# One-hots read from PSUM, first-expert tiles on two PSUM tiles, and a denser order of the last routing, in a retention and mixture-of-experts kernel

## The chip, the cores and the metric

The kernel runs on one core of a Trainium2 chip. The metric is the device time of one execution in microseconds, the median of the runs. A core has five engines that run side by side, each through its own list of instructions in order: TensorE (PE, with its weight loads PEld), VectorE (DVE), ScalarE (ACT), GpSimd (POOL) and SyncE (SP, which here only starts transfers).

## The reference

The kernel computes a retention layer and, from its output, a mixture of experts with two experts per token.

```python
B, H, S, D = 8, 8, 576, 64
scores = q @ k^T / sqrt(D)
gamma = 1 - 2 ** (-5 - h)                    # per head
ret = scores * where(i >= j, gamma ** (i - j), 0)
x = (ret @ v), as rows of 4608 tokens x 512
noisy = x @ w_gate + log1p(exp(x @ w_noise)) * noise      # 4608 x 8
top2 = the two largest of noisy per token; weights = softmax of those two
out[token] = sum over its two experts e: weight * (relu(x @ w1[e]) @ w2[e])   # 512 -> 1024 -> 512
```

## The kernel before

The work has three stages that overlap. **Attention** runs over 16 units (a unit is one batch, four heads), `n` from 0 to 16: unit `n` gets its scores while unit `n-1` gets its output (`out`). A unit's scores go through the PSUM tile `S` in two halves, each multiplied by a mask on DVE (L269) into SBUF. `cast` turns the loaded keys and queries into bf16 on POOL (`kn` at L199, `qb` at L207), two units ahead; `tr` transposes them on PE (L249); `states` (L288) writes the PSUM tile `T`. SP loads the units four ahead (L176, L181).

**Routing** works on 1152 tokens (two batches) at a time, four routings (`bp` from 0 to 3). `Router.route` is a generator: each `yield` ends a piece, and the main loop puts one piece between two parts of a unit (`step`). A routing computes the logits (PSUM tile `R`, L500), takes the two largest on DVE, counts ranks (running sums `cum` on POOL at L561, matmuls L600 and L602 into `R`), writes the token rows `xr` to DRAM (`xd`), and then builds the list of tokens for each slot of each expert: `olo` (L653) and `oh` (L657) are one-hot masks that DVE makes by comparing a row of column counts, `iota16` (0 to 127, f16, in SBUF), with numbers of each token. 18 matmuls (L668) of `oh` with `olo` add up the list in `R`. `finish` (L697, L698) makes `xi` of it, the row numbers for the gathers.

**Experts**: a tile is 256 slots of one expert. POOL gathers its two halves by an indirect transfer (`xd` by `xi`), PE transposes it, multiplies by `w1` (g1) and by `w2` (g2), and the result goes to `yd` or, with the token's first result added, to `out`. Five tiles whose slots are full early run ahead, in the generator `early` ("first-expert tiles" here, tile 0 to 4; L389 transposes, L398 g1 into the PSUM tile `S`, L402 relu on ACT, L411 g2, L414 the scaled copy `y`). They borrow the buffers `raw_q`, `raw_k`, `raw_v` of the attention loads, four of each name. Each g1 has eight column blocks of 128; a tile of `S` holds four. `early` yields after each relu and each g2 half, and one of its steps follows each piece of the last routing; it starts when three routings are done. Three of its tiles need two routings, the other two need three.

The 35 late tiles run in `experts`. The first three use `raw_q` buffers too (`pre`, L1214, L840), the others seven buffers `xg`. The buffers `xg` and `prv` (the token's first result) are set to zero once on DVE at the start of `experts` (L862, L864). The late tiles' small arithmetic (`small`, L920 to L931) stands on DVE ahead of the relu (L966); L943 transposes, L959 is their g1 and L979 their g2.

All five engines run in an order written out by hand (`manual_schedule`): instructions stand on each engine as the program emits them, so a late piece holds up what stands behind it.

Of the kernel before, what the change touches and what calls it, by code (L numbers as in the profile page):

```python
# [9 lines left out]
F16 = mybir.dt.float16  # L10
F32 = mybir.dt.float32
# [4 lines left out]
Act = mybir.ActivationFunctionType  # L16

P = 128
N = 4608
NCOL = N // P  # L20
E = 8
# [29 lines left out]
def constants(nc, cp):  # L51
    K = {}
    K["ident"] = cp.tile([P, P], BF16, name="ident")
    make_identity(nc, K["ident"])
    K["ones"] = cp.tile([P, P], BF16, name="ones")
    nc.vector.memset(K["ones"], 1.0)
    K["ltri"] = cp.tile([P, P], BF16, name="ltri")
    nc.vector.memset(K["ltri"], 1.0)
    nc.gpsimd.affine_select(K["ltri"], K["ltri"], pattern=[[1, P]], base=0, channel_multiplier=-1,
                            compare_op=Alu.is_gt, fill=0.0)  # L60
    K["iota"] = cp.tile([P, P], BF16, name="iota")
    nc.gpsimd.iota(K["iota"], pattern=[[1, P]], base=0, channel_multiplier=0,
                   allow_small_or_imprecise_dtypes=True)
    K["iota16"] = cp.tile([P, P], F16, name="iota16")
    nc.gpsimd.iota(K["iota16"], pattern=[[1, P]], base=0, channel_multiplier=0,
                   allow_small_or_imprecise_dtypes=True)
    K["local"] = cp.tile([P, NC9], F32, name="local")
    nc.gpsimd.iota(K["local"], pattern=[[P, NC9]], base=1, channel_multiplier=1,
                   allow_small_or_imprecise_dtypes=True)
    K["pidx"] = cp.tile([P, 1], F32, name="pidx")  # L70
    nc.gpsimd.iota(K["pidx"], pattern=[[0, 1]], base=0, channel_multiplier=1,
                   allow_small_or_imprecise_dtypes=True)
    K["desc"] = cp.tile([P, E], F32, name="desc")
    nc.gpsimd.iota(K["desc"], pattern=[[-1, E]], base=E, channel_multiplier=0,
                   allow_small_or_imprecise_dtypes=True)

    K["mask"] = cp.tile([P, 2, P], BF16, name="mask")
    nc.vector.memset(K["mask"], 1.0)
    for h in range(2):
        for rs in range(2):  # L80
            m = K["mask"][h * HD:(h + 1) * HD, rs, :].rearrange("p (r q) -> p r q", r=4)
            nc.gpsimd.affine_select(m, m, pattern=[[1, 4], [4, 32]], base=-rs, channel_multiplier=-2,
                                    compare_op=Alu.is_ge, fill=0.0)
    K["maskt"] = cp.tile([P, 2, HD], BF16, name="maskt")
    nc.vector.memset(K["maskt"], 0.0)
    for b in range(2):
        m = K["maskt"][b * HD:(b + 1) * HD, b, :]
        nc.vector.memset(m, 1.0)
        nc.gpsimd.affine_select(m, m, pattern=[[1, HD]], base=0, channel_multiplier=-1,
                                compare_op=Alu.is_ge, fill=0.0)  # L90

    K["tok"] = cp.tile([P, 4, NC9], F32, name="tok")
    for r in range(4):
        for b in range(2):
            nc.gpsimd.iota(K["tok"][r * 32:r * 32 + 32, :, 4 * b:4 * b + 4], pattern=[[1152, 4], [P, 4]],
                           base=r + 576 * b, channel_multiplier=4, allow_small_or_imprecise_dtypes=True)
    for h in range(2):
        t = K["tok"][h * HD:(h + 1) * HD]
        nc.gpsimd.iota(t[:, :, 8:9], pattern=[[1152, 4], [0, 1]], base=576 * h + 512, channel_multiplier=1,
                       allow_small_or_imprecise_dtypes=True)  # L100
    K["cols"] = cp.tile([P, NCOL], BF16, name="cols")
    nc.gpsimd.iota(K["cols"], pattern=[[1, NCOL]], base=1, channel_multiplier=0,
                   allow_small_or_imprecise_dtypes=True)

    K["cap"] = cp.tile([P, 3, E], F32, name="cap")
    for j, t in enumerate((CAPA, CAPB, ROW0)):
        for e in range(E):
            nc.gpsimd.memset(K["cap"][:, j, e:e + 1], float(t[e]))
    return K
# [250 lines left out]
def early(tc, K, at, keep, xd, yd, W, tiles, routed):  # L360
# [30 lines left out]

    def g1(i, fp):
        w = W[tiles[i][1]]
        p1 = at.ps.tile([P, 4, TS], F32, name="S", bufs=1)
        for f4 in range(4):
            for di in range(KD):
                o = di * F + (4 * fp + f4) * P
                nc.tensor.matmul(p1[:, f4, :], lhsT=w[:, o:o + P], rhs=st[i]["xT"][:, di, :],  # L398
                                 start=(di == 0), stop=(di == KD - 1))
            if f4 % 2:  # L400
                f = 4 * fp + f4 - 1
                nc.scalar.activation(st[i]["hT"][:, f:f + 2, :], p1[:, f4 - 1:f4 + 1, :], Act.Relu)  # L402
                yield

    def g2(i, s):
        n, e, t = tiles[i]
# [11 lines left out]

    for _ in range(3):
        gather(0)  # L420
    yield
    transp(0)
    yield
    for i in range(len(tiles)):
        for fp in range(KF // 4):
            for _ in g1(i, fp):
                gather(i)
                yield
        for s in range(2):
            if not s and i + 1 < len(tiles):  # L430
                while len(st) == i + 1:
                    yield
                    gather(i)
                transp(i + 1)
                yield
            g2(i, s)
            gather(i)
            yield


class Router:
    def __init__(self, tc, ctx, K, at, wgn, moe_noise, xd, keep):
# [11 lines left out]
        self.moe_noise = moe_noise  # L454
        self.w = self.one.tile([P, 2, NCOL], F32, name="w_all")
        self.ov = self.one.tile([P, 2, NCOL], F32, name="ov_all")

        self.fill = self.one.tile([P, 2, E], F32, name="fill")
        nc.vector.memset(self.fill, 0.0)
# [20 lines left out]
    def route(self, bp):  # L480
# [13 lines left out]
            nc.scalar.activation(xr[c // 3][:, c % 3, :DM // 2].bitcast(BF16), pt, Act.Copy)  # L494


        pg = ps.tile([P, C, 2, 2 * E], F32, name="R", bufs=1)
        for c in range(C):
            for di in range(KD):
                nc.tensor.matmul(pg[:, c].rearrange("p s e -> p (s e)"), lhsT=xT[:, di, c, :],  # L500
# [95 lines left out]
        G.tensor_copy(pl[:, :, 3], K["tok"][:, bp])  # L596
        yield
        row(6)
        pr = ps.tile(SH, F32, name="R", bufs=1)
        nc.tensor.matmul(pr.rearrange("p c a e -> p (c a e)"), lhsT=K["ltri"],  # L600
                         rhs=M.rearrange("p c a e -> p (c a e)"), start=True, stop=False)
        nc.tensor.matmul(pr.rearrange("p c a e -> p (c a e)"), lhsT=K["ones"],  # L602
# [47 lines left out]
        oh = sp.tile([P, 2, C, NH], F16, name="oh", bufs=1)  # L650
        for j in range(2):
            sh = [P, C, P]
            V.tensor_tensor(olo[:, j], K["iota16"].unsqueeze(1).to_broadcast(sh),  # L653
                            lo[:, j].unsqueeze(2).to_broadcast(sh), Alu.is_equal)
            yield
            for c in range(C):
                V.tensor_scalar(oh[:, j, c, :], K["iota16"][:, :NH], hi[:, j, c:c + 1], K["local"][:, c:c + 1],  # L657
                                Alu.is_equal, Alu.mult)
                if c == 4:
                    yield  # L660
            yield
        for a, t in ((self.keep["key"], rc.rearrange("p c a -> p a c")), (self.w, w), (self.ov, ov)):
            G.tensor_copy(a[:, :, c0:c0 + C], t)
        yield
        pT = ps.tile([P, NH], F32, name="R", bufs=1)
        for j in range(2):
            for c in range(C):
                nc.tensor.matmul(pT, lhsT=olo[:, j, c, :], rhs=oh[:, j, c, :],  # L668
# [16 lines left out]

    def counts(self, n):

        pn = self.at.ps.tile([P, 2, E], F32, name="R", bufs=1)
        self.nc.tensor.matmul(pn.rearrange("p a e -> p (a e)"), lhsT=self.K["ones"],
                              rhs=self.cum[:, n * NC9].rearrange("p a e -> p (a e)"), start=True, stop=True)  # L690
        return pn
# [153 lines left out]
def experts(tc, K, wp, w1, w2, keep, xd, yd, out, W, pre):  # L845
# [7 lines left out]
    with tc.tile_pool(name="moe_g", bufs=1) as gp, \  # L853
# [4 lines left out]
         tc.tile_pool(name="moe_ps", bufs=1, space=bass.MemoryType.PSUM) as ps:  # L858
        xgs = [gp.tile([P, 2, XW], F32, name=f"xg{j}") for j in range(NX)]
        prv = [gp.tile([P, 2, DM], F32, name=f"prv{j}") for j in range(NP)]  # L860
        for j in range(NX):
            nc.vector.memset(xgs[j], 0.0)  # L862
        for j in range(NP):
            nc.vector.memset(prv[j], 0.0)  # L864
        st = {}
        writes = []
        parts = {}
# [115 lines left out]

        def prev(i, s):
            if i < NT and seconds(i)[s]:
                rows = ROW0[LATE[i][0]]
                nc.gpsimd.indirect_dma_start(  # L987
                    out=prv[i % NP][:, s, :], out_offset=None, in_=yd[:rows, :],
                    in_offset=IOff(ap=st[i]["ix"][:, s, 1:2], axis=0),
                    bounds_check=rows - 1, oob_is_err=False)  # L990
# [40 lines left out]

        with tc.manual_schedule(engines=order):
            for i in range(len(pre), 5):
                for s in range(2):
                    gather(tc, keep, xd, xgof(i), i, s)
            small(0)
# [9 lines left out]
            for i in range(NT + 1):  # L1046
# [12 lines left out]
                if i + 1 >= NT:  # L1059
                    comb(i - 1)  # L1060

                for s in range(2):
                    if i + 5 < NT:
                        gather(tc, keep, xd, xgof(i + 5), i + 5, s)
# [28 lines left out]
def kernel(  # L1093
# [27 lines left out]
    with ExitStack() as actx, tc.manual_schedule(engines=order):  # L1121
# [21 lines left out]
            while work and next(work[0], work) is work:  # L1143
                work.pop(0)

        def step():
            while pend and next(pend[0], pend) is pend:
                pend.pop(0)
                routed.append(0)
                if len(routed) == 3:  # L1150
                    work.append(early(tc, K, at, keep, xd, yd, W, EARLY, routed))
            if n == NU:
                more()

# [6 lines left out]
        for n in range(NU + 1):  # L1161
# [40 lines left out]
                at.tr_tail((u + 1) // 4)  # L1202
            if n in (11, 12, 13, 14):
                load_weights(nc, wp, moe_w1, moe_w2, (n - 11) // 2, W, (n - 11) % 2)
            if n == NU - 1:
                more()
        while pend:
            step()
        rt.finish()

# [42 lines left out]
```

## Time and profile before

| What | us |
|---|---|
| Median of 3 runs | 531.49 (530.38 to 531.77) |
| Profiled execution, its time | 530.18 |
| Profiled execution, span of the trace | 528.3 |
| PE busy | 424.9 (80%) |
| ACT busy | 282.6 (53%) |
| POOL busy | 274.4 (52%) |
| DVE busy | 261.4 (49%) |
| L657 `oh`, 72 instructions, mean | 0.542 |
| L398 g1 of first-expert tiles, PE idle before it | 10.1 |

The page shows busy tenths of each engine in 40 slices of the span (13.2 us each). A timeline line reads: start, busy time, engine, line, operation, output and inputs with shapes, how many; in brackets how long the engine stood idle before it and what released it. Times in timelines count from the start of the span. Where several instructions of a line follow each other, they are shown as one with their number. The loop over the late tiles fills the span from about 257 us to 511 us.

### The profile page before, as it was taken

How to read it: one execution, taken by the hardware profiler on the slowest of the kernel's cores; microseconds unless marked ns; L12 is line 12 of the kernel's file. 1: busy time of each engine (PE TensorE's matmuls, PEld its weight loads, DVE VectorE, ACT ScalarE, POOL GpSimd, SP SyncE). 2: the span in 40 equal slices, each digit the busy share in tenths (PEclk: the TensorE clock that was granted, in tenths of full speed). 3: DMA queues.
4: the chain of work that ended last, by engine and by line, in shares of the span. 5: the costliest groups of instructions: out<-in, count | busy, mean ns of one | idle time of the engine just before them, and what ended most of it. 6: DMA issues, size and time to landing. Idle time of an engine off the chain costs nothing.

```text
span 528.3 us, 11736 instructions
## 1 busy us (share of the span) xinstructions
PE 424.9 (80%) x4627; PEld 304.3 (58%) x4627; DVE 261.4 (49%) x695; ACT 282.6 (53%) x429; POOL 274.4 (52%) x379
## 2 busy tenths in 40 slices
PE   0477677477277758787999999999999999999960
PEld 0365555366266535564767676676666776666630
DVE  4343298868956854724233433424434354444440
ACT  3487597398449326544456666575655744322200
POOL 3783357327733153508505571744747767777440
PEclk9998677686767658999999999999999999999995
DMA  8996899992853821334677698697797864645330
GB/s 245 261 241 167 211 241 308 255 309 57 181 86 61 174 55 59 96 106 113 212 254 254 229 302 280 216 338 227 274 348 249 293 242 141 205 157 176 134 125 2
DMA packets 96169, 104.19 MB, mean 197 GB/s; under 512 B 25447, under 2 KB 73064, under 8 KB 96112
## 3 DMA queue, kind: packets, MB, share of 16 engines
q1 hardware_dynamic: 79824, 69.51, 44.2%
q0 software_dynamic: 14176, 32.83, 22.3%
q10 hardware_dynamic: 2112, 1.08, 0.7%
q8 instruction: 37, 0.61, 0.5%
q14 instruction: 20, 0.16, 0.1%
HBM read 84.66 MB, written 28.72 MB: 215 GB/s over the span
## 4 chain that ended last, share of the span: by engine, by line
PE 55%; ACT 3%; DVE 3%; POOL 2%; issue 2%; DMA 2%; POOLq 0%; DVEq 0%
PE po L979 23%; PE p L959 23%; PE S L398 3%; PE pt L943 3%; PE x L411 2%; ACT raw_k L402 1%; POOL xg L840 1%; POOL raw_q L840 1%; DMA xg<-xd,xi 1%; DMA raw_q<-xd,xi 1%; DMA out_dram<-o,ix 1%; ACT xr L494 0%; DVE olo L653 0%; DVE S L269 0%; DVE oh L657 0%
## 5 line engine op out<-in xcount | busy, mean ns | idle before, releaser
L959 PE MATMUL p<-xgT,w 128*128 128x256 bf16 x1120 | 211.3, 273 | 0.7 <-DVE hT L966 0.7
L979 PE MATMUL po<-w,hT 128*128 128x512 bf16 x560 | 209.8, 379 | 0.0
L959 PEld LDWEIGHTS <-w 128*128 128x128 bf16 x1120 | 109.5, 98 | 71.1 <-issue 0.9
L966 DVE TENSOR_SCALAR hT<-p 128x512 bf16<-128x512 f32 x70 | 48.3, 692 | 142.3 <-PE p L959 142.3
L964 ACT ACTIVATE hT<-p 128x512 bf16<-128x512 f32 x70 | 41.8, 597 | 120.8 <-PE p L959 95.7
L1025 POOL DMA_INDIRECT out_dram<-o,ix x45 | 45.6, 1013 | 61.1 <-DVE o L1019 47.4
L840 POOL DMA_INDIRECT xg<-xd,xi x64 | 65.1, 1017 | 18.7 <-issue 13.2
L269 DVE TENSOR_TENSOR S<-S,mask 128x1024 bf16<-128x1024 f32 x32 | 39.1, 1222 | 49.5 <-PE S L264 49.5
L987 POOL DMA_INDIRECT prv<-yd,ix x45 | 45.1, 1002 | 31.7 <-DMA yd<-y 18.3
L979 PEld LDWEIGHTS <-hT 128*128 128x128 bf16 x560 | 54.8, 98 | 7.5
L909 ACT ACTIVATE w<-wst 128x1024 bf16<-128x1024 f32 x48 | 47.8, 1047 | 0.0
L199 POOL TENSOR_TENSOR kn<-raw_k,kg 128x1024 bf16<-128x1024 f32 x14 | 26.6, 1899 | 40.7 <-DMA raw_k<-in_k_dram 21.0
L264 PE MATMUL S<-QT,KT 64*64 64x128 bf16 x512 | 17.5, 274 | 23.4 <-DVE S L269 15.2
L946 ACT ACTIVATE xgT<-pt 128x1024 bf16<-128x1024 bf16 x35 | 35.6, 1017 | 1.4 <-PE pt L943 1.4
L1019 DVE SCALAR_TENSOR_TENSOR o<-po,g,prv 128x512 f32<-128x512 f32 x45 | 31.6, 742 | 0.8 <-PE po L979 0.8
L398 PE MATMUL S<-raw_v,w 128*128 128x256 bf16 x160 | 23.5, 296 | 10.1 <-ACT raw_k L402 9.0
L207 POOL TENSOR_TENSOR qb<-raw_q,qg 128x1024 bf16<-128x1024 f32 x14 | 28.8, 2058 | 0.0
L264 PEld LDWEIGHTS <-KT 64*64 64x64 bf16 x512 | 11.2, 134 | 28.0 <-issue 17.8
L249 PE MATMUL tr<-ident,qb 128*128 128x128 bf16 x128 | 14.2, 278 | 16.2 <-DVE qb L207 12.8
L657 DVE TENSOR_SCALAR oh<-iota,hi,local 128x80 f16<-128x80 f16 x72 | 26.9, 542 | 0.0
L204 ACT ACTIVATE vn<-raw_v 128x1024 bf16<-128x1024 f32 x16 | 16.8, 1052 | 18.7 <-DMA raw_v<-in_v_dram 12.7
L398 PEld LDWEIGHTS <-w 128*128 128x128 bf16 x160 | 16.8, 105 | 15.9 <-issue 12.8
(212 smaller groups left out, 636.7 us busy)
## 6 DMA issues: line engine op xcount, KB each, us to landing
wst<-in_moe_w_dram SPq DMA_DIRECT2D x48, 512.0 KB, 6.1
raw_k<-in_k_dram SPq DMA_DIRECT2D x32, 256.0 KB, 5.9
raw_v<-in_v_dram SPq DMA_DIRECT2D x32, 256.0 KB, 6.6
yd<-y SPq DMA_DIRECT2D x16, 512.0 KB, 3.6
raw_q<-in_q_dram SPq DMA_DIRECT2D x14, 512.0 KB, 6.0
xd<-xr SPq DMA_DIRECT2D x12, 396.0 KB, 4.6
w<-in_moe_w_dram POOLq DMA_DIRECT2D x4, 1024.0 KB
yd<-raw_v SPq DMA_DIRECT2D x5, 512.0 KB, 3.4
```

What stands on the lines that cost most here:

```text
L269: nc.vector.tensor_tensor(S.rearrange("p h c r t -> p (h c) (r t)"), p.rearrange("p h (c r) t -> p (h c) (r t)", r=2), self.K["mask"].rear ...
L398: nc.tensor.matmul(p1[:, f4, :], lhsT=w[:, o:o + P], rhs=st[i]["xT"][:, di, :], start=(di == 0), stop=(di == KD - 1))
L840: tc.nc.gpsimd.indirect_dma_start(out=xg[:, s, :], out_offset=None, in_=xd[:, :], in_offset=IOff(ap=keep["xi"][:, j:j + 1], axis=0), bound ...
L909: nc.scalar.activation(W[e][:, k * F:(k + 1) * F], t, Act.Copy)
L946: return lambda: nc.scalar.activation(xgT, pt, Act.Copy)
L959: nc.tensor.matmul(p1[:, f2, :], lhsT=w[:, o:o + P], rhs=xgT[:, di, :], start=(di == 0), stop=(di == KD - 1))
L964: nc.scalar.activation(hT[:, 2 * fp:2 * fp + 2, :], p1, Act.Relu)
L966: V.tensor_relu(hT[:, 2 * fp:2 * fp + 2, :], p1)
L979: nc.tensor.matmul(po[s], lhsT=hT[:, fi, s * P:(s + 1) * P], rhs=w[:, o:o + DM], start=(fi == 0), stop=(fi == KF - 1))
L987: nc.gpsimd.indirect_dma_start(out=prv[i % NP][:, s, :], out_offset=None, in_=yd[:rows, :], in_offset=IOff(ap=st[i]["ix"][:, s, 1:2], axis=0),
L1019: V.scalar_tensor_tensor(o[:, s, :], st[i]["po"][s], st[i]["g"][:, s:s + 1], prv[i % NP][:, s, :], Alu.mult, Alu.add)
L1025: ins = nc.gpsimd.indirect_dma_start(out=out[:, :], out_offset=IOff(ap=st[i]["ix"][:, s, 0:1], axis=0), in_=st[i]["o"][:, s, :], in_offset ...
```

## The change

The column counts are copied once from `iota` into a part of a PSUM bank as f32, and both one-hot masks read them there. The bank is now one tile for the whole attention stage: logits and ranks, lists, counts and the column counts have each their own columns of it. g1 of the first-expert tiles goes in four groups of two column blocks, in turn into the PSUM tile `T` and `S`, with one relu and one `yield` for each; each of its first three gathers is now a step of its own. `early` starts at the end of unit slot `n` = 14 instead of after the third routing, with a step at `n` = 14 and 15 and in every `step` of `n` = 16. From `n` = 14 on there is one piece of routing more per slot, and after the last slot two pieces to each step of `early`. The zeroing of `xg` and `prv` moves from DVE to POOL, each just before the first transfer into the buffer.

```diff
-    K["iota16"] = cp.tile([P, P], F16, name="iota16")
-    nc.gpsimd.iota(K["iota16"], pattern=[[1, P]], base=0, channel_multiplier=0,
-                   allow_small_or_imprecise_dtypes=True)
...
     def g1(i, fp):
         w = W[tiles[i][1]]
-        p1 = at.ps.tile([P, 4, TS], F32, name="S", bufs=1)
-        for f4 in range(4):
+        p1 = at.ps.tile([P, 4, TS] if fp % 2 else [P, 2, TS], F32, name="S" if fp % 2 else "T", bufs=1)
+        for f2 in range(2):
             for di in range(KD):
-                o = di * F + (4 * fp + f4) * P
-                nc.tensor.matmul(p1[:, f4, :], lhsT=w[:, o:o + P], rhs=st[i]["xT"][:, di, :],
+                o = di * F + (2 * fp + f2) * P
+                nc.tensor.matmul(p1[:, f2, :], lhsT=w[:, o:o + P], rhs=st[i]["xT"][:, di, :],
                                  start=(di == 0), stop=(di == KD - 1))
-            if f4 % 2:
-                f = 4 * fp + f4 - 1
-                nc.scalar.activation(st[i]["hT"][:, f:f + 2, :], p1[:, f4 - 1:f4 + 1, :], Act.Relu)
-                yield
+        nc.scalar.activation(st[i]["hT"][:, 2 * fp:2 * fp + 2, :], p1[:, :2], Act.Relu)
...
     for _ in range(3):
         gather(0)
-    yield
+        yield
...
-        for fp in range(KF // 4):
-            for _ in g1(i, fp):
-                gather(i)
-                yield
+        for fp in range(KF // 2):
+            g1(i, fp)
+            gather(i)
+            yield
...
+        bank = self.bank = at.ps.tile([P, 512], F32, name="R", bufs=1)
+        self.iota = bank[:, 384:]
+        nc.vector.tensor_copy(self.iota, K["iota"])
...
-        pg = ps.tile([P, C, 2, 2 * E], F32, name="R", bufs=1)
+        pg = self.bank[:, :C * 4 * E].rearrange("p (c s e) -> p c s e", c=C, s=2)
...
-        pr = ps.tile(SH, F32, name="R", bufs=1)
+        pr = self.bank[:, :C * 2 * E].rearrange("p (c a e) -> p c a e", c=C, a=2)
...
-            V.tensor_tensor(olo[:, j], K["iota16"].unsqueeze(1).to_broadcast(sh),
+            V.tensor_tensor(olo[:, j], self.iota.unsqueeze(1).to_broadcast(sh),
...
-                V.tensor_scalar(oh[:, j, c, :], K["iota16"][:, :NH], hi[:, j, c:c + 1], K["local"][:, c:c + 1],
+                V.tensor_scalar(oh[:, j, c, :], self.iota[:, :NH], hi[:, j, c:c + 1], K["local"][:, c:c + 1],
...
-        pT = ps.tile([P, NH], F32, name="R", bufs=1)
+        pT = self.bank[:, 288:288 + NH]
...
-        pn = self.at.ps.tile([P, 2, E], F32, name="R", bufs=1)
+        pn = self.bank[:, 368:368 + 2 * E].rearrange("p (a e) -> p a e", a=2)
...
-        for j in range(NX):
-            nc.vector.memset(xgs[j], 0.0)
-        for j in range(NP):
-            nc.vector.memset(prv[j], 0.0)
+        fresh = set()
+
+        def clear(t, j):
+
+            if (t is xgs, j) not in fresh:
+                fresh.add((t is xgs, j))
+                nc.gpsimd.memset(t[j], 0.0)
...
             if i < NT and seconds(i)[s]:
+                clear(prv, i % NP)
...
             for i in range(len(pre), 5):
+                clear(xgs, i % NX)
...
+                if i + 5 < NT:
+                    clear(xgs, (i + 5) % NX)
...
-        def step():
+        def piece():
             while pend and next(pend[0], pend) is pend:
                 pend.pop(0)
                 routed.append(0)
-                if len(routed) == 3:
-                    work.append(early(tc, K, at, keep, xd, yd, W, EARLY, routed))
+
+        def step():
+            piece()
             if n == NU:
                 more()
...
-            if n == NU - 1:
+            if n >= NU - 2:
+                piece()
+
+            if n == NU - 2:
+                assert len(routed) >= 2
+                work.append(early(tc, K, at, keep, xd, yd, W, EARLY, routed))
+            if n in (NU - 2, NU - 1):
                 more()
         while pend:
+            piece()
             step()
```

## The prediction

> **What bounds the kernel now.** I read the busy slices first, then stage sums from the windows view, then the timeline of each engine where a stage had holes.
>
> ```profile
> PE   0477677477277758787999999999999999999960
> DVE  4343298868956854724233433424434354444440
> PEclk9998677686767658999999999999999999999995
> ```
>
> ```profile
> 87.00:187.00 100.00, 66.08 (x1282) 51.22 (x1279) 77.92 (x192) 60.70 (x94) 44.41 (x74) 0.70 0.71 166
> 187.00:257.00 70.00, 53.33 (x432) 36.55 (x433) 33.34 (x127) 34.09 (x54) 35.99 (x59) 0.89 0.30 90
> 257.00:520.00 263.00, 253.70 (x1903) 175.19 (x1901) 107.62 (x287) 130.23 (x173) 147.37 (x148) 0.99 0.69 232
> ```
>
> (Columns: stretch, length, busy us of PE, PEld, DVE, ACT, POOL, clock, DMA share, GB/s.) From 257 us PE is busy 253.7 of 263 us at clock 0.99: this is the loop over the 35 late tiles, nothing in the change touches its PE work, and it only starts earlier or later. Before 87 us the waits of the casts are for the loads of `raw_k` (21.0 us in five waits, the last ending at 65 us). So the change acts in 87 to 257 us.
>
> The DVE timeline shows two large holes that belong to the one-hots of routings 0 and 1:
>
> ```profile
> 87.72 2.53 DVE L653 TENSOR_TENSOR olo<-iota,lo 128x1152 f16<-128x1152 f16 x1
> 90.17 6.96 DVE L657 TENSOR_SCALAR oh<-iota,hi,local 128x80 f16<-128x80 f16 x9
> 97.05 1.35 DVE L653 TENSOR_TENSOR olo<-iota,lo 128x1152 f16<-128x1152 f16 x1
> 98.31 1.21 DVE L269 TENSOR_TENSOR S<-S,mask 128x1024 bf16<-128x1024 f32 x1
> 99.45 1.98 DVE L657 TENSOR_SCALAR oh<-iota,hi,local 128x80 f16<-128x80 f16 x9
> ...
> 134.15 7.97 DVE L657 TENSOR_SCALAR oh<-iota,hi,local 128x80 f16<-128x80 f16 x9
> ```
>
> ```profile
> 87.13 1.90 POOL L199 TENSOR_TENSOR kn<-raw_k,kg 128x1024 bf16<-128x1024 f32 x1
> 89.00 3.01 POOL L207 TENSOR_TENSOR qb<-raw_q,qg 128x1024 bf16<-128x1024 f32 x1
> ...
> 92.49 1.90 POOL L199 TENSOR_TENSOR kn<-raw_k,kg 128x1024 bf16<-128x1024 f32 x1
> ```
>
> ```profile
> L657 DVE TENSOR_SCALAR oh<-iota,hi,local x72: 286/299/4855, 90.2 to 224.1; 128x80 f16<-128x80 f16 x72
> ```
>
> ```profile
> 99.58 0.64 PE L264 MATMUL S<-QT,KT 64*64 64x128 bf16 x16 [6.89 <-DVE S L269]
> ```
>
> Nine one-hots take 1.98 us alone and 6.96 or 7.97 us beside POOL's casts; one of them took 4855 ns. `S` stands behind them on DVE, and PE's next scores wait for it.
>
> In 187 to 257 us the first-expert tiles lose time at one PSUM tile, and the end of the stretch hangs on POOL's gathers:
>
> ```profile
> PE S L398 <- ACT raw_k L402: 9.0, 15, 0.8
> ```
>
> ```profile
> 236.18 1.04 POOL L840 DMA_INDIRECT raw_q<-xd,xi  x1 [12.56 <-DVE fill L713]
> ...
> 251.47 1.00 POOL L840 DMA_INDIRECT raw_q<-xd,xi  x1 [0.30 <-issue]
> ```
>
> ```profile
> 254.40 0.17 DVE L920 TENSOR_SCALAR isB<-raw_q 128x2 f32<-128x2 f32 x1 [7.52 <-POOL key L709]
> ```
>
> The last routing's index list `xi` is done at 235.43 us. Late tile 2 is gathered by the 11th and 12th transfers of POOL after it, the last issued at 251.47; `small(2)` follows at 254.40 and holds back `hT` on DVE and PE behind it.
>
> **The change part by part.** All against the profiled execution: span 528.3, time 530.18, which is 1.3 below the median of the runs (531.49).
>
> *One-hots from PSUM, routings 0 and 1.* A gain needs that a DVE read of PSUM is not held up by POOL. Rows for it: `S<-S,mask` reads PSUM and one SBUF operand and never takes over 1.23 us, also where a POOL cast runs beside it:
>
> ```profile
> 35.30 1.23 DVE L269 TENSOR_TENSOR S<-S,mask 128x1024 bf16<-128x1024 f32 x1 [1.62 <-PE S L264]
> ```
>
> ```profile
> 34.22 1.90 POOL L199 TENSOR_TENSOR kn<-raw_k,kg 128x1024 bf16<-128x1024 f32 x1 [2.24 <-PE T L288]
> ```
>
> [...] No row shows the new one-hot itself. Its price: `s<-R` (L674, 128x80 from PSUM, two immediates) takes 230 ns; a pointer operand costs about 48 ns (L1007 with one 740, L966 without 692, both 128x512 from PSUM); so 326 ns where it is 286 now. I take +60 ns, 0.5 us for nine. [...] Below zero is excluded: nothing makes an undisturbed one faster. The `olo` mask stays at 1.35 (S: 1222 ns for 1024, plus 128 elements).
>
> Routing 0: from 87.72, `olo` 1.26 (97.05 to 98.31), nine one-hots 2.45, `olo` 1.26: `S` at 92.7 for 98.31, 5.6 us earlier. Routing 1: from 131.70 to 136.7 for 143.25, 6.55 earlier.
>
> Taken back: constants, logits, ranks and lists now lie in one bank `R`. In the built order only the first of the 18 list matmuls (L668) still waits for DVE, and for all 18 one-hots; today each of the later ones waits for its own. [...] Behind that matmul on PE stand the `kn` transposes, the second nine and `scores_tail` (L338). Today L338 starts 4.3 us after `S`; new: mask 1.14, one-hots 2.45, matmuls and transposes 2.2, so 5.8. That is 1.5 us back, twice. Sum: 5.6 + 6.55 - 3.0 = 9.1. [...] What is late next: `kn` and `qb` for the following units are done by 96.3 or earlier, the loads for units 12 to 15 were issued by 118 and are used after 114, 125, 131 and 139, so nothing new binds.
>
> *Routing 2, units 15 and 16.* POOL does nothing there in the trace, so no stall goes. One-hots end at 183.9 (183.7 today), and PE, which now waits for the last of them, starts the lists at 184 instead of 179. `xi` comes at about 188 (187.6 today). Six gathers of first-expert rows and three memsets (9.5 us) move into POOL's idle time at 174 to 185, so tile 0 needs no gather chain after that; PE can transpose it at 185 (191.6 today). But tile 0's four groups stand on PE ahead of the last logits (L500): at half clock some 1.9 us each, at full 0.9. Logits end at about 195.7 for 188.8: **7 us late.**
>
> *The last routing.* Two pieces for each first-expert step. From 195.7: `lg` 0.65, exponent, table load 1.28 and log to 198.6 (today 198.7, for ACT is in order). Eleven memsets (3.5 + 3.6 us) leave DVE, 1.8 of them between here and `M`: `M` at 202.5. The exponent of `d` stands behind two `y`, two relu and five row copies instead of all of tile 0 and 1: 204.7 for 210.97. Its ranks wait for POOL's nine sums (2.7): 205.7. Then 1.9 ranks, 1.6 lists, 7.45 one-hots (6.6 today): 216.6. PE has by then 1.7 us left of g1, then lists: L at 218.7, `xi` at 219.9; I add 1.1 for hand-overs: **221 for 235.43, 14.4 us earlier.** Today PE runs the lists 9.74 us after the one-hots because they stand behind first-expert groups; that goes.
>
> *First-expert tiles on two PSUM tiles.* A group takes 1.72 us (239.21 to 240.93), of that 0.69 waiting; alternating, 0.87 (half of a 16-matmul g2, 3.47). A tile: 7.4 us. After the lists PE has 0.87 + 0.45 + 3.45 + 2 x 7 + 0.45 = 19 us left, done at 239: this is cover, not the end.
>
> *Memsets on POOL.* The end is POOL: late tile 2 needs the buffer of first-expert tile 3, so it now stands behind fourteen gathers, four xg memsets (0.56 + 0.27 in place of the 0.30 gap), one of `prv` (about 1.05) and the two raw ones. From `xi`: 0.75 + 14 x 1.31 + 5 x 0.55 + 1.1 + 0.6 = 23.2 to the first, 24.5 to the second, landing 2.9 later as today: `xi` + 27.4, where today it is `xi` + 19.0. **8.4 us back.** So late tile 2 at 248.4 for 254.40, and PE waits some 3 us at its transposes: a gain of 6.0. The remaining `prv` and `xg` memsets lie in the 18.3 us that POOL waits for `yd`; the weights' loads (SP, behind `key`) come at `xi` + 27 and are needed later than before relative to it.
>
> *Constants.* One POOL iota goes (0.24), one DVE copy comes (0.3 at 9.9 us). Cost nothing: the casts wait for `raw_k` at 22 and 45 us.
>
> **Sum:** 9.1 + 6.0 = 15.1: 515.1 for the profiled execution, 516.4 for the median. I say 516.
>
> **The rivals.**
> 1. *The reads from PSUM are still held up* (pointer operands lie in SBUF). Routings 0 and 1 then lose 3 us instead of winning 9; total 3 faster: 528. Against it: `S` under POOL. 0.10.
> 2. *POOL does not bind*: the last gathers land under PE's 19 us, because the list ends sooner or PE's clock stays low longer. The late tiles then start as PE is free, 9 to 11 earlier: 510. For: 3 us lie between the two. 0.20.
> 3. *POOL's queue turns the end round*: if the last routing's `xi` is no earlier than today in its own stage (the logits' 7 us and the half clock not recovered), the extra gathers and memsets cost 8.4 in full and more where a memset waits for its buffer. With 9 from the one-hots it decides at `xi` 0.6 us later than 235.43; at 3 later, 534. Against: 9.74 us of PE order vanish at the lists. 0.06.
> 4. *The new bound is the one-hots' price*: half the gain of routings 0 and 1 lost, two routings longer: 521. 0.14.
>
> Forecast as summed: 0.50.
>
> **The numbers.** 0.3% (1.6 us) is what a measurement can tell. Faster: forecast, 1, 2 and 4 less a little: 0.91; within 0.03; slower 0.06. The range takes 6 to 12 for the one-hots and 1 to 10 for the second part: 509 to 524.
>
> **What would show it.** Right: `oh` with a maximum under 450 ns and median near 330; `S` after routing 0 at about 92.7; PE's wait of 6.89 under 3; PE waits for ACT at L398 gone; logits of routing 3 late against the `out` of the last unit, its `xi` 14 us sooner; PE idle at the transposes of late tile 2 with POOL's gathers before it; the late loop unchanged at 7.39 us a tile. Wrong: `oh` still in the microseconds; `xi` no earlier; a late loop with new waits for `prv` or `xg`.

## The result and the profile after

| | before | after |
|---|---|---|
| Median, us | 531.33 (530.38 to 531.77, 4 runs) | 515.65 (515.48 to 516.98, 4 runs) |
| Ratio, 95% interval | | 0.9713 [0.9692, 0.9734] |
| Profiled execution: time, span | 530.18, 528.3 | 516.98, 515.2 |
| DVE busy, POOL busy, PE busy | 261.4, 274.4, 424.9 | 248.4, 278.9, 420.6 |

The profiled execution of after is the longest of its four; the spans of the other three lie between 513.6 and 513.8. Three stretches of after follow, cut roughly where the same work begins and ends as in the stretches of before (columns as there: stretch, length, busy us of PE, PEld, DVE, ACT, POOL, clock, DMA share, GB/s), and under them the busy tenths of its page.

```profile
87.00:180.00 93.00, 65.39 (x1260) 52.19 (x1261) 67.21 (x189) 61.33 (x94) 49.85 (x82) 0.69 0.82 189
180.00:242.00 62.00, 49.06 (x428) 34.99 (x433) 28.28 (x119) 33.31 (x53) 32.62 (x58) 0.97 0.33 100
242.00:507.00 265.00, 253.66 (x1869) 175.95 (x1902) 110.05 (x288) 130.21 (x173) 149.85 (x150) 0.98 0.68 227
```

```profile
PE   0576777687589487895999999999999999999960
DVE  4333288658847838611233434534434445444440
```

The last stretch has the same PE work as before (253.66 us against 253.70). The two stretches ahead of it are some 7 and 8 us shorter. DVE is busy 10.7 us less in the first of them.

The one-hots on DVE, from the timeline, and then the line's durations (minimum, median and maximum in ns):

```profile
87.61 1.35 DVE L651 TENSOR_TENSOR olo<-R,lo 128x1152 f16<-128x1152 f32 x1
88.87 2.50 DVE L655 TENSOR_SCALAR oh<-R,hi,local 128x80 f16<-128x80 f32 x9
...
92.56 1.21 DVE L266 TENSOR_TENSOR S<-S,mask 128x1024 bf16<-128x1024 f32 x1
```

```profile
L655 DVE TENSOR_SCALAR oh<-R,hi,local x72: 343/350/354, 88.9 to 207.4; 128x80 f16<-128x80 f32 x72
```

The spread from 286 to 4855 ns has become one from 343 to 354. Nine one-hots take 2.50 us everywhere, and the mask of `S` starts at 92.56 us instead of 98.31. What PE does with that, from its timeline in the same slot, with the lists of the last two routings under it:

```profile
93.82 0.42 PE L261 MATMUL S<-QT,KT 64*64 64x128 bf16 x16 [2.36 <-DVE S L266]
96.24 0.76 PE L666 MATMUL R<-oh,olo 128*128 128x80 f16 x9 [2.00 <-DVE oh L655]
...
176.88 0.76 PE L666 MATMUL R<-oh,olo 128*128 128x80 f16 x9 [4.71 <-DVE oh L655]
...
207.79 0.76 PE L666 MATMUL R<-oh,olo 128*128 128x80 f16 x9 [3.59 <-DVE oh L655]
```

PE's wait for `S` is 2.36 us instead of 6.89, and a wait for `oh` at the first list matmul is new in the first routing: that is the common bank. Over the four routings these waits are 2.00, 1.84, 4.71 and 3.59 us, 12.1 in all, against 1.9 before. In e2 and e3 below, where the bank is shared as here but the counts lie in SBUF, they are nearly gone (1.0 us in all in e3 and 2.2 in e2, where the first nine lists of the last routing start at 208.36 us, while one-hots are made until 211): what makes the lists wait for all one-hots is that the one-hots read the bank into which the lists are written. Then the way from the last `xi` to the loop over the late tiles, from the timelines of DVE, POOL and PE:

```profile
211.82 0.24 DVE L696 SCALAR_TENSOR_TENSOR xi<-L,z 128x80 int32<-128x80 f32 x1
```

```profile
212.82 1.04 POOL L838 DMA_INDIRECT raw_q<-xd,xi  x1 [7.84 <-DVE big L717]
...
237.01 1.01 POOL L838 DMA_INDIRECT raw_q<-xd,xi  x1 [0.30 <-issue]
```

```profile
239.92 0.17 DVE L922 TENSOR_SCALAR isB<-raw_q 128x2 f32<-128x2 f32 x1 [9.33 <-DMA raw_q<-xd,xi]
```

```profile
238.74 0.38 PE L945 MATMUL pt<-ident,raw_q 128*128 128x128 bf16 x4 [1.89 <-POOL key L707]
239.84 0.40 PE L945 MATMUL pt<-ident,raw_q 128*128 128x128 bf16 x4 [0.71 <-DMA raw_q<-xd,xi]
...
242.09 0.59 PE L961 MATMUL p<-xgT,w 128*128 128x256 bf16 x2 [1.85 <-DVE hT L968]
```

`xi` is done at 212.06 us (before 235.43). The last gather of late tile 2 is issued at 237.01, `small(2)` stands at 239.92 (before 254.40), and PE has three holes of 4.45 us in all ahead of the loop.

### The profile page after: what moved, and what is told of

It reads as the page before. It is cut to its first block, busy times and chain, and to the rows that moved or that the text cites. A ratio compares the mean times of both kernels' runs of the same rounds, so it can differ in the third digit from the quotient of the medians.

```text
span 515.2 us, 11707 instructions
## 1 busy us (share of the span) xinstructions
PE 420.6 (82%) x4587; PEld 304.6 (59%) x4627; DVE 248.4 (48%) x685; ACT 282.6 (55%) x429; POOL 278.9 (54%) x389
## 4 chain that ended last, share of the span: by engine, by line
PE 52%; DVE 6%; POOL 3%; issue 3%; DMA 1%; ACT 1%; POOLq 0%; DVEq 0%
PE p L961 24%; PE po L981 22%; PE pt L945 3%; DVE oh L655 2%; POOL xg L838 1%; DVE olo L651 1%; PE T L395 1%; PE x L405 1%; POOL raw_q L838 1%; DMA raw_q<-xd,xi 1%; DMA out_dram<-o,ix 1%; DVE S L266 0%; POOL xg L865 0%; PE R L666 0%; ACT raw_v L387 0%
## 5 line engine op out<-in xcount | busy, mean ns | idle before, releaser
L981 PE MATMUL po<-w,hT 128*128 128x512 bf16 x525 | 197.8, 381 | 0.1
L961 PEld LDWEIGHTS <-w 128*128 128x128 bf16 x1120 | 109.9, 98 | 72.9 <-issue 3.0
L559 POOL TENSOR_TENSOR cum<-cum,M 128x16 bf16<-128x16 bf16 x36 | 8.2, 228 | 36.9 <-DVE d L562 34.4
L261 PE MATMUL S<-QT,KT 64*64 64x128 bf16 x512 | 17.1, 268 | 12.3 <-ACT KT L248 7.2
L204 POOL TENSOR_TENSOR qb<-raw_q,qg 128x1024 bf16<-128x1024 f32 x14 | 26.6, 1900 | 0.0
L285 PE MATMUL T<-vn,kn 64*64 64x64 bf16 (+2 forms) x512 | 25.3, 243 | 0.0
L491 PE MATMUL tr<-ident,xT 128*128 128x128 bf16 x144 | 17.8, 262 | 8.6 <-ACT xr L492 8.1
L492 ACT ACTIVATE xr<-tr 128x512 bf16<-128x512 bf16 x36 | 21.3, 594 | 3.8 <-issue 2.9
```

The source lines that it names most:

```text
L961: nc.tensor.matmul(p1[:, f2, :], lhsT=w[:, o:o + P], rhs=xgT[:, di, :], start=(di == 0), stop=(di == KD - 1))
L981: nc.tensor.matmul(po[s], lhsT=hT[:, fi, s * P:(s + 1) * P], rhs=w[:, o:o + DM], start=(fi == 0), stop=(fi == KF - 1))
```

## The experiments

To compare kernels that ran on different chips I use the *front* of each profile: from the mask of `S` in the first half of unit slot 7 (at 82 to 84 us everywhere) to the first relu of the steady loop on DVE (the `hT` whose successor follows 3.47 us later). From that relu to the end of the span it is 268.0 to 268.1 us in before, in after and in the first eight kernels below; so the front holds all that the change does. It is 177.3 us before and 164.2 after (about 162.8 for the other three executions of after, whose spans are 1.4 us shorter). Each front is one execution. Two fronts can differ without a cause in the kernel: e7 and e10 are the same program up to the last `xi`, on two chips, and reach it 132.4 and 134.6 us after the start of their fronts. So differences of 2 us say nothing.

The last four kernels shared a chip on which the loop over the late tiles took 317 to 320 us instead of 268 and the kernel before 593.71; of these I read the front. Their medians and ratios are comparable only with one another: on this chip the kernel before, which has no trace there, is slower by 62 us, and e9 to e12 save 28 to 39 us by medians where the fronts account for 17 to 26.

| Kernel | Median, us | Ratio to before, 95% | Front |
|---|---|---|---|
| e1 before + one-hots from PSUM | 524.73 | 0.9864 [0.9797, 0.9931] | 171.2 |
| e2 after, counts f16 in SBUF | 522.29 | 0.9835 [0.9769, 0.99] | 168.6 |
| e3 after, counts f32 in SBUF | 524.26 | 0.9871 [0.9804, 0.9938] | 170.6 |
| e4 after, late tiles 1 and 2 in `xg` | 509.08 | 0.9587 [0.952, 0.9654] | 157.0 |
| e5 after, zeroing on DVE | 515.07 | 0.9728 [0.9708, 0.9747] | 162.0 |
| e6 after, g1 on one PSUM tile | 518.12 | 0.9801 [0.9765, 0.9836] | 165.3 |
| e7 after, one piece to a step | 506.14 | 0.9567 [0.9533, 0.9602] | 152.6 |
| e8 after, lists one piece later | 511.77 | 0.9663 [0.9628, 0.9698] | 158.1 |
| e9 e4 + e7 + e8 | 554.90 | 0.9354 [0.9317, 0.9391] | 151.0 |
| e10 e4 + e7 | 560.75 | 0.9441 [0.9387, 0.9494] | 156.1 |
| e11 after, main loop of before | 563.75 | 0.9501 [0.9447, 0.9555] | 160.3 |
| e12 e8 + idle transposes | 565.24 | 0.9541 [0.9501, 0.9581] | 160.7 |

**e1: the one-hots alone.** The kernel before, with the bank `R`, the copy of the counts and the two masks as in the change:

```diff
-            V.tensor_tensor(olo[:, j], K["iota16"].unsqueeze(1).to_broadcast(sh),
+            V.tensor_tensor(olo[:, j], self.iota.unsqueeze(1).to_broadcast(sh),
...
-                V.tensor_scalar(oh[:, j, c, :], K["iota16"][:, :NH], hi[:, j, c:c + 1], K["local"][:, c:c + 1],
+                V.tensor_scalar(oh[:, j, c, :], self.iota[:, :NH], hi[:, j, c:c + 1], K["local"][:, c:c + 1],
```

> The kernel before with one part of the change alone: column counts as f32 in the PSUM bank R, both one-hot masks read there, logits, ranks and lists in the same bank. Early tiles, routing order and memsets as before. My theory (the stalls beside POOL's casts go, the common bank gives some back): oh with a maximum under 400 ns, S after routing 0 at about 92.6 us and after routing 1 at about 135, time 522 to 525 (the prediction's sum for this part is 9.1 us; the trace of after has 7.2 us left of it when routing 2 makes its list). Rival 1 (the gain comes from the order of the last routing, and what the one-hots save is eaten by the bank wait and the half clock): 528 to 531. Rival 2 (PSUM reads are held up too): oh in the microseconds, 531 or more.

Measured 524.73 beside 530.99 of the kernel before: 6.3 us. The stalls are gone (maximum 353 ns). Rivals 1 and 2 fall; but the prediction's 9.1 was 3 too much.

**e2 and e3: place or type.** After, with the counts in SBUF again, once as f16 and once as f32:

```diff
+    K["iota16"] = cp.tile([P, P], F16, name="iota16")
+    nc.gpsimd.iota(K["iota16"], pattern=[[1, P]], base=0, channel_multiplier=0,
+                   allow_small_or_imprecise_dtypes=True)
...
-        self.iota = bank[:, 384:]
-        nc.vector.tensor_copy(self.iota, K["iota"])
+        self.iota = K["iota16"]
```

(e3 has `iota32` and `F32` in its place.)

> The changed kernel with the one-hots' column counts in SBUF as f16 again; the bank R and everything else as changed. My theory: oh has a maximum of several microseconds again beside POOL's qb, the two routings lose 7 to 9 us, time 522 to 525. Rival (the order of the last routing is what pays, the stall is hidden by it): 516 to 518.

> The changed kernel with the column counts in SBUF but as f32. Tells the place from the type. If it is the place (PSUM instead of SBUF) that keeps DVE out of POOL's way: oh still has a maximum in the microseconds and the time is as with f16 in SBUF, 522 to 525. [...] For olo (two SBUF inputs in either case) I expect about 2.5 us beside POOL in both.

The one-hot's line in e2 and in e3:

```profile
L657 DVE TENSOR_SCALAR oh<-iota,hi,local x72: 285/296/4824, 90.0 to 210.9; 128x80 f16<-128x80 f16 x72
```

```profile
L657 DVE TENSOR_SCALAR oh<-iota,hi,local x72: 303/311/4762, 90.0 to 213.6; 128x80 f16<-128x80 f32 x72
```

Both have maxima of 4.8 us: it is the place, not the type. The type costs 15 ns (296 to 311), the place 39 more (311 to 350), all by medians. Taking PSUM out of the change costs 6.6 us by medians (8.6 as f32), about what putting it in alone brought. `olo`, with two SBUF inputs, takes 2.54 us beside POOL in e2 and 1.35 from PSUM.

**e4: POOL's order after `xi`.** Only late tile 0 takes a buffer `raw_q`; tiles 1 and 2 take `xg`, which are free.

```diff
-        for i in range(3):
+        for i in range(1):
             xg = raw.tile([P, 2, 4, P], F32, name="raw_q").rearrange("p c h w -> p (c h w)")[:, :2 * XW].rearrange(
```

> The changed kernel, but only late tile 0 is gathered into a buffer of the attention stage (raw_q); late tiles 1 and 2 go into xg buffers, so that no gather of a late tile waits in POOL's list behind all fourteen gathers of the first-expert tiles. My theory (POOL's order sets the start of the late loop in the changed kernel: small(2) at xi + 27.9 us, PE idle 3.6 us and then about 3 us at half clock): the late tiles' small arithmetic comes 5 us or more sooner, PE goes from g2 of the last first-expert tile into the late loop without a hole, 4 to 5 us faster than the changed kernel: 510 to 512. Rival (the hole is DVE's or SP's, such as the weights' loads behind key): 515 to 516, with the hole at the same place. Second rival (the loads of the later tiles then come late instead): 513 to 518 with new waits for xg in the loop.

Measured 509.08, 6.6 us under after. POOL and PE in e4:

```profile
215.12 1.06 POOL L838 DMA_INDIRECT xg<-xd,xi  x1 [0.17 <-issue]
...
216.72 1.02 POOL L838 DMA_INDIRECT xg<-xd,xi  x1 [0.16 <-issue]
```

```profile
229.67 0.61 PE L945 MATMUL pt<-ident,raw_q 128*128 128x128 bf16 x8 [0.78 <-ACT raw_v L408]
231.44 0.61 PE L945 MATMUL pt<-ident,xg 128*128 128x128 bf16 x8 [1.16 <-ACT xgT L948]
```

The gathers of late tile 1 are the third and fourth after `xi`, those of late tile 2 the fifth and sixth (issued by `xi` + 9.8; in after the last of them came at `xi` + 25), and PE goes into the loop without a hole that DMA or POOL ends. So in after POOL's order does hold the start back.

**e5: the zeroing on DVE.**

```diff
+        for j in range(NX):
+            nc.vector.memset(xgs[j], 0.0)
+        for j in range(NP):
+            nc.vector.memset(prv[j], 0.0)
```

(and nothing in `clear`.)

> The changed kernel with the zeroing of xg and prv on DVE at the start of the experts again. My theory (POOL's list from xi to the gathers of late tile 2 sets the start of the late loop, and the memsets put 3 to 4 us into it; on DVE they cost 1.8 us ahead of the last routing's M): small(2) at xi + 24.5 instead of xi + 27.9, xi 0 to 2 us later, time 512.5 to 515 against 515.65 of the changed kernel. Rival (DVE's time in the last routing counts in full and PE, not POOL, ends last): 516 to 519.

Measured 515.07; the interval covers the ratio of after: no difference. Counted from the start of `xi`, `small(2)` comes after 25.5 us instead of 28.1, but `xi` itself starts 2.2 us later (214.00 for 211.82). What POOL's list loses, the last routing on DVE gains. So moving the memsets to POOL is worth nothing either way; by e4 it is the order of the gathers that holds the start back.

**e6: one PSUM tile for g1.**

```diff
-        p1 = at.ps.tile([P, 4, TS] if fp % 2 else [P, 2, TS], F32, name="S" if fp % 2 else "T", bufs=1)
+        p1 = at.ps.tile([P, 4, TS], F32, name="S", bufs=1)
```

> The changed kernel with the four g1 groups of a first-expert tile all on the one PSUM tile S (in place of T and S in turn). My theory (the prediction's: PE's work under POOL's gathers is cover): groups 1.7 us apart instead of 0.87, PE waits for the relu at L395 again, some 0.85 us for each of 20 groups, of which about 10 stand after xi: PE is free some 8 us later, at xi + 27 and near POOL's xi + 28, time 515.5 to 519. Rival (alternating the tiles is what pays): 522 or more.

Measured 518.12, as expected: 2.5 us by medians, 4.7 by ratios, and 1.1 to 2.5 by fronts. PE comes to the first late transposes at 238.35 us instead of 230.99, and the loop starts only a little later, since POOL held it anyway. In the order of after most of what the second tile saves PE is hidden behind POOL.

**e7: one piece to a step.** The edit that overturned my reading:

```diff
         while pend:
-            piece()
             step()
```

> The changed kernel with one piece of the last routing to each first-expert step after the last slot, as before (the second piece taken out; everything else as changed). My theory (xi of the last routing starts POOL's chain, which ends xi + 28 us later): xi 6 to 10 us later than 212.1, and the time 5 to 10 us over the changed kernel: 521 to 526. Rival (PE's own work sets the start of the late loop, so that the order of pieces only moves slack): 515 to 517.

Both theories fall. `xi` is 3.2 us later, and the time is not longer but **9.5 us shorter** by medians, 7.8 by ratios (the two kernels ran on different chips): 506.14. Two stretches of after (from routing 2's list to `xi`, and from there to the first late g1) and the same two of e7:

```profile
181.00:212.00 31.00, 24.52 (x245) 17.95 (x245) 18.57 (x75) 18.86 (x33) 10.34 (x31) 0.94 0.27 92
212.00:233.00 21.00, 18.91 (x138) 12.40 (x139) 7.56 (x32) 12.33 (x18) 16.49 (x19) 1.00 0.38 112
```

```profile
178.00:215.00 37.00, 35.96 (x344) 25.92 (x343) 18.42 (x75) 26.81 (x45) 10.36 (x31) 1.00 0.29 100
215.00:226.00 11.00, 6.86 (x52) 4.26 (x51) 5.86 (x28) 4.44 (x7) 8.34 (x9) 0.99 0.39 120
```

The sum of PE's work is nearly the same, 43.4 and 42.8 us. In after the routing's pieces come so densely that PE stands still for 6.5 of the 31 us before `xi`, the longest time (3.59 us) for the one-hots, and 19 us of first-expert work are left after it. In e7 each gap of the routing has enough of that work in it: PE is idle for 1.0 of 37 us. When `xi` comes, PE is nearly through, the buffer of first-expert tile 3 is free, and late tile 2's gathers are the 7th and 8th after `xi` instead of the 15th and 16th. What is then left, from e7's timelines:

```profile
229.36 0.27 DVE L922 TENSOR_SCALAR isB<-raw_q 128x2 f32<-128x2 f32 x1 [1.84 <-DMA raw_q<-xd,xi]
```

```profile
224.68 0.38 PE L945 MATMUL pt<-ident,raw_q 128*128 128x128 bf16 x4 [3.18 <-DMA raw_q<-xd,xi]
```

`small(2)` stands at `xi` + 14, and one wait of PE for a gather is left. The shorter time has two causes that come together in this run: PE has less work left after `xi`, and late tile 2's gathers stand earlier in POOL's list. e4 removes the second alone and gives 6.6 us (6.7 by ratios); e10 below adds it to e7.

**e8: the bank wait.** The lists of the first two routings stand one piece later, behind the `kn` transposes. The first nine list matmuls still stand ahead of `scores_tail`, the second nine now behind it.

```diff
+        if bp < 2:
+            yield
         pT = self.bank[:, 288:288 + NH]
```

> The changed kernel with the first two routings' 18 list matmuls emitted one piece later (one extra yield ahead of them), so that on PE the kn transposes and scores_tail stand ahead of the matmul that waits for all one-hots of the common bank. My theory (that bank wait gives back about 1.5 us in each of the two routings): PE's waits of 2.00 and 1.84 us for oh ahead of the lists go or no longer stand before scores_tail, 1 to 3 us faster than the changed kernel: 512.5 to 514.5. Rival (scores_tail then only waits for DVE, where its mask stands behind the same one-hots, and the half clock takes the rest): 515 to 516.

Measured 511.77: 3.9 us by medians, 2.7 by ratios, the first a little more than expected. The two slots differ. In the first the wait for `oh` falls from 2.00 to 1.45 us, `scores_tail` then waits for DVE, and by 113 us only 0.2 us are gained:

```profile
97.16 0.76 PE L668 MATMUL R<-oh,olo 128*128 128x80 f16 x9 [1.45 <-DVE oh L655]
98.29 0.40 PE L335 MATMUL S<-TT 64*128 64x128 bf16 x4 [0.37 <-DVE S L266]
```

The second (wait 1.03 instead of 1.84) gains 2.1 us by the next unit's scores and 3.6 by 165 us, counted from its own first scores; the clock of 150 to 165 us is 0.89 instead of 0.77.

**e10 and e9: do the gains add?** e10 joins e4 and e7; e9 joins e8 as well.

> The changed kernel with one piece to each first-expert step and late tiles 1 and 2 in xg buffers. Tells apart why one piece alone gave 9.5 us. Theory A (only POOL's order: with the first-expert tiles done sooner, late tile 2's gathers move up in POOL's list, which the xg buffers do as well): no faster than the better of the two alone, 506 to 509. Theory B (PE: two pieces at a time make PE wait for the routing between too little first-expert work, so that 19 us of that work are left after xi where one piece leaves 5): the xg buffers come on top, since POOL's hole after xi is then what is left: 502 to 504.5.

> The changed kernel with three edits together: one piece of the last routing to each first-expert step, late tiles 1 and 2 gathered into xg buffers, lists of the first two routings one piece later. If their gains add as far as the traces allow (one piece: 9.5 us, of which the order of POOL's gathers is a part; lists: 3.9; xg buffers: then only PE's remaining wait of 3.2 us and the half clock after it, 2 to 3): 499 to 502. Rival (one piece and xg buffers are the same gain, and the hole after xi stays): 502 to 505.

With their fronts, e10 and e9 would take 509.6 and 504.5 us on the chip of e7 (an estimate: 506.14 of e7, plus the difference of the fronts). So e10 is no better than e7, as theory A had it: the `xg` buffers add nothing to e7. Of the 3.5 us by which its front is longer, 2.2 lie ahead of `xi`, where the two are the same program; from the start of `xi` to the loop e10 takes 21.5 us and e7 20.2. That A's reason, the order of gathers alone, is all of e7's gain is not shown: PE's idle time in e7's first stretch above speaks against it. After `xi`, PE waits elsewhere in e10. POOL now has the arithmetic of `key` and the zeroing of `xg` between the first eight gathers, so the eighth is issued at `xi` + 12.6 instead of + 10.9, and on DVE the first `hT` stands behind the arithmetic of the fourth late tile, which waits for it.

```profile
232.51 0.17 DVE L922 TENSOR_SCALAR isB<-xg 128x2 f32<-128x2 f32 x1 [1.74 <-DMA xg<-xd,xi]
```

```profile
234.78 0.38 PE L961 MATMUL p<-xgT,w 128*128 128x256 bf16 x2 [1.72 <-DVE hT L968]
```

e8 does add: e9's front is 5.1 us under e10's on the same chip, of which 4.6 lie ahead of `xi`. e9 has the smallest front of all, but only 1.6 us under e7's, which ran on another chip, so that this order is not shown; e7 is the fastest measured on a chip with the loop at 268 us. e7 with e8 and without the `xg` buffers was not tried.

**e11: the main loop of before.** After, with first-expert tiles from the third routing on, no extra pieces, one piece to a step:

```diff
+                if len(routed) == 3:
+                    work.append(early(tc, K, at, keep, xd, yd, W, EARLY, routed))
...
-            if n >= NU - 2:
-                piece()
...
-            if n in (NU - 2, NU - 1):
+            if n == NU - 1:
                 more()
         while pend:
-            piece()
             step()
```

> The changed kernel with the main loop of the kernel before: first-expert tiles start when three routings are done, no extra pieces in the slots from n = 14 on, one piece to a step. What is left of the change is the one-hots in PSUM, the two PSUM tiles of g1, a step for each of the first gathers, and the zeroing on POOL. If the start at n = 14 is what pays beside the one-hots: 519 to 523 (the one-hots alone gave 524.7, alternating the tiles some 2.5 more). Rival (the start is worth little, the rest does it): 506 to 512.

Front 160.3: 7.7 us behind e7, 10.9 ahead of e1. With e7's time that would be some 514 us on the ordinary chip (an estimate as above), which is neither expectation. The early start is worth 7.7 beside one piece to a step: `xi` comes 133.0 us after the start of the front (132.4 in e7), and from the start of `xi` to the loop it takes 27.3 us instead of 20.2. Against e1, `xi` comes 12.3 us earlier. Most of that I put down to the two PSUM tiles, which were worth 2.5 us by medians in e6; this is read from PE's waits and not shown by a run, since the zeroing and the steps of the gathers differ too. From PE's waits in e1, after 178 us (total, times, longest):

```profile
PE S L395 <- ACT raw_k L399: 9.2, 15, 0.8
```

In e11 there is no such row.

**e12: the clock.** e8, with the transposes of two units done four times into the same tile. The copies only repeat work.

```diff
-        for hp in range(2):
+        for hp in [0, 1] * (4 if u in (8, 12) else 1):
```

> The changed kernel with the lists of the first two routings one piece later (511.8 us when run alone), and besides in the two slots of those routings each block of transposes of q and k done four times into the same tile, 48 transposes more in a slot, some 1.3 us for 24 at full clock. They do nothing but keep PE at work while it would wait for S and for the one-hots. Theory (after such a wait PE runs at half clock for several microseconds: granted clock 0.50 at 97 to 105 and 110 to 115 us; that took back 2 us of the first routing's gain): the clock stays near 1 after the slot, 508 to 511. Rival (the clock falls anyhow, the extra work costs): 512.5 to 515.

Its front is 2.6 us longer than e8's, but on another chip, where 2.2 us have been seen without a cause; and it gives no answer: the copies fell one slot too early and not into the wait that they were to fill.

```profile
125.72 2.97 PE L246 MATMUL tr<-ident,qb 128*128 128x128 bf16 x30
...
136.45 0.42 PE L261 MATMUL S<-QT,KT 64*64 64x128 bf16 x16 [2.09 <-DVE S L266]
```

Whether work in the wait would hold the clock stays open.

## Why the prediction was right, point by point

- **One-hots, mechanism: right.** These reads from PSUM were not held up: the longest one-hot took 353 ns in e1 and 354 in after, against 4824 in e2 and 4762 in e3, which read SBUF. `S` at 92.56 was predicted at 92.7. The price was +58 ns by the undisturbed groups of nine (1.98 to 2.50 us), +54 by the medians of e2 and after, close to the +60 of the forecast, for which rows of the trace gave +40 (326 for 286). No run shows a price behind the range's ends of 6 and 12 us for this part: the runs showed +54 to +58, and the 6.3 us of e1 are put down to another term (next point). Rival 1 falls, and the price that rival 4 was built on was not paid.
- **One-hots, size: too large.** Predicted 9.1, measured 6.3 in e1 and 7.2 in after where routing 2 makes its list (180.37 for 187.6). The failing term is "1.5 us back, twice". The bank wait is there (2.00 and 1.84 us), but what follows was not in the sum: PE works at half clock after it (0.50 in both stretches of after). Before and after in the same two stretches:

```profile
97.00:105.00 8.00, 5.21 (x84) 4.20 (x83) 6.46 (x16) 1.40 (x2) 0.33 (x1) 0.57 1.02 216
110.00:115.00 5.00, 3.10 (x82) 2.53 (x83) 2.31 (x11) 4.98 (x8) 0.00 (x0) 0.92 1.14 309
```

```profile
97.00:105.00 8.00, 8.00 (x155) 6.32 (x153) 2.97 (x7) 3.19 (x6) 3.77 (x2) 0.50 1.11 238
110.00:115.00 5.00, 5.00 (x98) 4.16 (x95) 2.87 (x9) 4.32 (x9) 0.00 (x0) 0.50 1.12 313
```

  The 4.2 us won at the first `scores_tail` (98.39 for 102.61) are 1.9 by 113 us. That the half clock is the cause is read from these rows and not shown: e8 moved both, e12 missed.
- **Routing 2: right in kind.** No stall goes; the logits end at 186.96 (before 188.86). With the shift of 7.2 taken off, that is 5.3 us late, predicted 7.
- **Last routing: right.** 9.1 + 14.4 = 23.5 us for `xi`, measured 23.4; its two parts are 7.2 and 16.2, so the second was too small by what the first was too large. That the sum fits so closely is luck. The 9.74 us by which the lists came after the one-hots are gone; in their place PE waits 3.59 us for the one-hots.
- **POOL's list after `xi`: right in size, half right in cause.** `small(2)` at `xi` + 27.9 (predicted 27.4; the terms as listed add up to 23.5 and not 23.2 us to the first gather, so 27.7). PE stands still 4.45 us ahead of the loop, where some 3 were predicted. e4 shows that this list sets the start: rival 2's case, in which POOL does not bind and for which 510 was predicted, is what e4 makes, with 509.08. But the heading "memsets on POOL" names the wrong part: without them (e5) nothing is gained. The gathers ahead of tile 2 are the price.
- **Two PSUM tiles as cover: right for this order.** PE is free 18.2 us after `xi` (predicted 19); e6 costs 2.5 by medians. The group took 0.87 us as predicted, which is a quarter of the 3.47 us of a g2 and not half. In e11's order the tiles seem to be worth more.
- **What the prediction did not see.** It counted the second piece to a step only as the 14.4 us it brings for `xi`. It also left PE 19 us of work for after `xi`, called cover in the text; e7 shows that without the second piece that work fits into the routing's own gaps. The sum was right for the kernel as written; but the second piece, to which it gave much of the 14.4 us, costs 9.5 us by medians (7.8 by ratios).
- **Sum.** 15.1 us were predicted, 15.7 measured by medians. Fronts, of one execution each and not all on one chip, give the change as a chain: 177.3, one-hots 171.2 (e1), two PSUM tiles with the zeroing and the gathers' own steps 160.3 (e11), early start with the extra piece in slots 14 and 15 152.6 (e7), second piece 164.2 (after). Gains of 6, 11 and 8 and a loss of 12. Of that loss 1.4 us may belong to after's profiled execution alone: its first 3 us of the loop ran at a granted clock of 0.50 (0.63 us a pair of matmuls instead of 0.38), and the other three executions are 1.4 us shorter, but have no trace that would show whether it is this.

## What to carry to other kernels

Interleave a latency-bound chain with independent work so that each gap of the chain is filled: emitting the chain more densely makes its result earlier, but when the same in-order engine has to do the other work afterwards, an earlier result (here by 3.2 us) can end later (here by 9.5 us by medians, 7.8 by ratios). Before you call work behind a result "cover", ask whether it could have been done ahead of it. An operand that moves from SBUF to PSUM can take DVE out of POOL's way (here the longest one-hot took 354 ns instead of 4855) at a small price per instruction (here 54 ns), but what is written into its bank then waited for all its readers (here 12.1 us of PE's time instead of 1.9).

## What the runs showed of the hardware that I had not expected

- **PE was busy for 8 us without a break and stayed at half clock.** In after the profile has it busy 8.00 of 8.00 us from 97 to 105 at 0.50 (the ends of matmuls are modelled there). Why is open, and so is what a stall of 2 us costs in this way.
- **The same loop took 51 us longer on another chip** (319 us in e9, 268 in e7). A stretch of the late loop in e9 and one of the same length in e7:

```profile
350.00:450.00 100.00, 86.16 (x577) 55.69 (x586) 34.46 (x97) 44.07 (x57) 51.56 (x51) 0.90 0.61 200
```

```profile
300.00:400.00 100.00, 100.00 (x756) 69.50 (x755) 44.09 (x118) 59.71 (x78) 62.07 (x62) 1.00 0.83 280
```

  PE is idle for 14 of 100 us, mostly in gaps that no semaphore ends (from PE's waits in the loop of e9: total, times, longest):

```profile
PE p L963 <- issue: 13.4, 21, 1.6
PE po L983 <- issue: 10.3, 14, 1.1
```

  The stages ahead of the loop had nearly their usual times there. The cause is open; the kernel before is slower there as well (593.71), so it is none of the change's.
